# The first MLP product by seven products for eight, four tiles at once, in half of the features of blocks 2 to 6

## The chip, the cores and the metric

The kernel runs on one core of a Trainium2 chip. A core has five engines with a queue each, which work in the order of their queues and wait for one another by semaphores: TensorE (PE in the profile; its weight loads are PEld), VectorE (DVE), ScalarE (ACT), GpSimd (POOL) and SyncE (SP, which here only issues DMAs). Matrix products land in PSUM, 8 banks of 128 partitions by 512 words of 32 bits. The metric is the device time of one execution in microseconds (us), the median of three runs.

## The reference

An attention with random features is followed by an MLP. For q, k, v of shape (8 batches, 8 heads, 576 positions, 64) and omega of 128 x 64:

```python
q_p, k_p = phi(q * scale), phi(k * scale)      # exp(projection - norm - max), 128 features
num = q_p @ (k_p^T v);  den = q_p . sum(k_p)   # per batch and head
x = (num / den) as 4608 tokens x 512
h = x @ w_in                                   # 512 x 2048
g = h * clip(h + 3, 0, 6) / 6
out = g @ w_out                                # 2048 x 512
```

## The kernel before, in words

**Blocks and stages.** The tokens are worked in nine blocks of 512: block b (0 to 7) is the main 512 positions of batch b, block 8 holds the 64 left over of each batch. Stage b holds three things that the engines interleave: the attention of batch b + 1 (projections on TensorE, exponentials on ScalarE, maxima and divisions on VectorE, scaling of v on GpSimd or ScalarE), the first MLP product of block b, and the second MLP product of block b - 1.

**First product, eight for eight.** `mm1` (L1048 on) makes one tile of 128 features by 512 tokens: four matmuls of 512 columns at L1064 into one PSUM bank. ScalarE then makes relu(h/6 + 0.5) into `tsb` (L1070), and VectorE multiplies min(tsb, 1) with the bank into `gT` (L1072). A block has 16 such tiles.

**First product, seven for eight.** In blocks 7 and 8 `mm1_pair` is used instead (`FIRST7 = (7, 7)`, one number for each half of the features). It takes features f and f + 8 and both halves of the tokens as a 2 x 2 product and makes it with seven products of half the size in place of eight, from sums and differences of the tokens (`x_sums`: X1 to X4) and of the weights (`input_sums`: W1 to W4). It has 14 matmuls of 256 columns at L1143. Partial results are copied from one PSUM bank to another (or to `p7` in SBUF) by ScalarE or VectorE (256 columns each), and a later matmul adds onto the copy: [...]such a bank (`onto`) must have held a full tile. Two additions on VectorE (L1180, L1182) follow.

**Second product.** From block 1 on it is made with seven products for eight as well: `token_sums` and `last_sum` form S1 to S4 of `gT`, four sums for each quarter of the features, and `products` (L1322) has 7 x 16 matmuls of 256 columns. All sums of the kernel pass through `combine` (L1250). S1 to S4 run on GpSimd (`ADD`), except in the last block, where VectorE shares them.

**Order.** Each engine's order is written out by hand in `ORDER`, as numbers of operations. A small planner (`schedule`) walks these lists with assumed durations. It decides only which PSUM bank each tile gets and which semaphore waits are needed; the engines then run freely.

**Buffers.** The sums of weights and tokens for the first product lie in the space of `k32` and `q32`, which only batch 0 uses for its own data.

Of the kernel before, what the change touches and what calls it, by code (L numbers as in the profile page):

```python
# [14 lines left out]
IDLE_UNTIL = 21.0  # L15
EV0 = (("ACT","DVE"), ("ACT","DVE"), ("POOL", "ACT"), {"k": ("POOL", "ACT", "DVE"), "q": ("POOL", "ACT","DVE")})
# [6 lines left out]
        240, 223, 395, 396, 408, 238, 245, 401, 402, 403, 397, 225, 398, 213, 404, 409, 243, 410, 413, 416, 271, 198,  # L23
        419, 251, 228, 422, 425, 428, 291, 431, 434, 275, 273, 277, 279, 437, 303, 300, 440, 294, 309, 297, 306, 443,
        446, 449, 287, 289, 576, 315, 283, 596, 566, 567, 322, 597, 568, 330, 285, 312, 577, 281, 324, 578, 357, 569,
        326, 579, 328, 336, 318, 580, 320, 598, 332, 570, 344, 334, 581, 571, 586, 587, 346, 359, 349, 582, 362, 599,
        583, 383, 588, 370, 572, 589, 388, 375, 600, 372, 385, 352, 590, 591, 592, 365, 378, 601, 391, 593, 602, 603,
        614, 620, 573, 629, 493, 503, 505, 617, 632, 495, 623, 501, 466, 469, 472, 644, 635, 638, 499, 509, 653, 475,
        511, 507, 478, 650, 481, 490, 484, 647, 665, 487, 497, 659, 775, 668, 662, 519, 776, 521, 531, 785, 536, 524,
        533, 778, 779, 543, 708, 555, 545, 548, 786, 560, 557, 791, 788, 789, 688, 792, 794, 795, 701, 798, 799, 808,  # L30
        715, 802, 817, 820, 805, 811, 728, 832, 823, 733, 835, 740, 730, 826, 847, 841, 745, 838, 853, 742, 963, 856,
        752, 850, 754, 764, 979, 757, 964, 766, 973, 769, 966, 967, 974, 876, 976, 977, 980, 889, 982, 983, 993, 996,
        1005, 990, 1008, 999, 986, 987, 916, 1011, 896, 1023, 1020, 1014, 903, 1026, 928, 1029, 1041, 1035, 933, 930,
        1044, 940, 1151, 921, 1038, 945, 918, 1152, 952, 942, 1167, 957, 954, 1161, 1154, 1162, 1077, 1155, 1164,
        1165, 1064, 1168, 1170, 1171, 1084, 1184, 1181, 1193, 1178, 1187, 1174, 1175, 1091, 1202, 1104, 1199, 1214,
        1116, 1196, 1118, 1106, 1208, 1217, 1109, 1121, 1229, 1140, 1226, 1211, 1145, 1128, 1223, 1133, 1130, 1232,
        1339, 1349, 1340, 1142, 1355, 1265, 1342, 1343, 1350, 1272, 1356, 1352, 1353, 1381, 1369, 1372, 1384, 1366,
        1375, 1358, 1362, 1359, 1363, 1396, 1252, 1405, 1387, 1399, 1390, 1411, 1417, 1402, 1420, 1414, 1304, 1292,
        1527, 1297, 1279, 1528, 1294, 1306, 1309, 1543, 1316, 1537, 1318, 1530, 1321, 1531, 1538, 1328, 1453, 1330,
        1333, 1540, 1541, 1460, 1544, 1546, 1467, 1550, 1547, 1551, 1440, 1554, 1563, 1560, 1557, 1572, 1492, 1584,  # L40
        1497, 1494, 1480, 1575, 1482, 1485, 1516, 1569, 1518, 1504, 1590, 1509, 1521, 1506, 1587, 1578, 1593, 1605,
        1599, 1602, 1608, 1622, 1623, 1653, 1666, 1625, 1656, 1682, 1669, 1658, 1626, 1671, 1695, 1661, 1685, 1632,
        1674, 1687, 1711, 1698, 1633, 1700, 1724, 1690, 1714, 1635, 1716, 1636, 1703, 1727, 1753, 1740, 1719, 1729,
        1641, 1642, 1743, 1756, 1732, 1745, 1800, 1758, 1638, 1639, 1748, 1803, 1813, 1761, 1805, 1645, 1646, 1816,
        1808, 1829, 1818, 1769, 1770, 1832, 1842, 1821, 1834, 1858, 1772, 1845, 1773, 1847, 1837, 1861, 1779, 1871,
        1863, 1850, 1887, 1780, 1874, 1866, 1900, 1876, 1890, 1782, 1783, 1892, 1879, 1903, 1785, 1786, 1905, 1788,
        1895, 1789, 1908, 1932, 1916, 1917, 1792, 1793, 1926, 1927, 1919, 1920, 1929, 1930, 1933, 1951, 1936, 1937,
        1948, 1945,
    ],
    "SP": [  # L50
        0, 18, 22, 33, 20, 23, 26, 25, 24, 27, 28, 32, 29, 30, 31, 262, 260, 261, 465, 464, 462, 461, 463, 460, 459,
        687, 575, 393, 685, 585, 684, 686, 595, 539, 605, 527, 551, 563, 681, 682, 564, 683, 801, 873, 872, 874, 736,
        797, 869, 875, 748, 760, 772, 870, 773, 871, 1060, 989, 985, 1062, 1063, 1057, 1061, 936, 924, 1059, 960, 948,
        1058, 961, 1248, 1249, 1250, 1251, 1246, 1177, 1124, 1112, 1136, 1148, 1149, 1245, 1247, 1173, 1433, 1361,
        1365, 1436, 1438, 1439, 1437, 1312, 1300, 1435, 1324, 1336, 1337, 1434, 1549, 1500, 1553, 1488, 1524, 1512,
        1525, 1644, 1648, 1791, 1795, 1939, 1943, 1953, 1941, 1950,
    ],
    "ACT": [
        21, 19, 118, 139, 132, 148, 142, 160, 145, 136, 151, 128, 124, 154, 184, 167, 157, 134, 187, 202, 169, 175,
        173, 171, 163, 179, 232, 219, 177, 165, 234, 181, 209, 224, 399, 405, 411, 414, 214, 199, 417, 272, 229, 420,  # L60
        423, 252, 426, 292, 432, 429, 276, 435, 274, 278, 438, 301, 295, 310, 441, 298, 307, 444, 304, 288, 450, 284,
        447, 356, 323, 290, 316, 313, 286, 343, 282, 331, 358, 327, 337, 319, 325, 333, 321, 329, 335, 345, 381, 369,
        384, 584, 371, 353, 366, 379, 392, 604, 594, 615, 621, 574, 504, 494, 506, 618, 633, 496, 624, 502, 630, 470,
        467, 645, 636, 473, 639, 500, 654, 510, 476, 651, 482, 479, 485, 648, 518, 491, 666, 488, 660, 514, 530, 669,
        498, 520, 663, 508, 532, 777, 541, 512, 554, 780, 544, 711, 556, 714, 709, 713, 693, 689, 697, 695, 700, 694,
        691, 702, 706, 707, 704, 723, 699, 721, 809, 720, 803, 716, 821, 718, 727, 806, 812, 738, 833, 818, 824, 741,
        750, 827, 842, 836, 839, 751, 762, 848, 763, 753, 854, 851, 857, 965, 885, 879, 887, 882, 883, 877, 565, 890,
        892, 888, 911, 894, 994, 881, 997, 1006, 895, 991, 914, 1000, 1009, 1012, 897, 902, 899, 927, 901, 1021, 1015,
        904, 906, 1024, 909, 929, 1030, 939, 1027, 951, 1036, 1042, 908, 950, 1045, 1039, 1153, 953, 1082, 1078, 1080,
        1083, 1067, 1070, 1073, 1071, 1075, 1115, 1069, 1065, 1076, 1085, 1087, 1185, 1182, 1089, 1090, 1179, 1194,  # L70
        1102, 1092, 1188, 1203, 1105, 1094, 1097, 1200, 1117, 1197, 1127, 1215, 1096, 1139, 1209, 1218, 1212, 1129,
        1230, 1227, 1224, 1233, 1341, 1268, 1271, 1266, 1270, 1275, 1277, 1278, 1273, 1370, 1373, 1367, 1385, 1376,
        1382, 1397, 1255, 1253, 1261, 1263, 1388, 1257, 1264, 1259, 1303, 1400, 1391, 962, 1406, 1412, 1403, 1258,
        1418, 1291, 1421, 1415, 1314, 1282, 1280, 1315, 1285, 1529, 1284, 1326, 1532, 1329, 1458, 1459, 1454, 1456,
        1461, 1463, 1466, 1465, 1472, 1473, 1470, 1468, 1441, 1443, 1449, 1445, 1447, 1446, 1555, 1452, 1561, 1558,
        1564, 1493, 1515, 1479, 1573, 1451, 1481, 1576, 1517, 1585, 1505, 1570, 1579, 1588, 1594, 1591, 1600, 1606,
        1603, 1609, 1624, 1654, 1655, 1667, 1668, 1657, 1670, 1683, 1662, 1684, 1627, 1664, 1675, 1696, 1697, 1677,
        1699, 1712, 1713, 1691, 1693, 1715, 1704, 1725, 1726, 1720, 1706, 1728, 1741, 1754, 1742, 1733, 1755, 1722,
        1744, 1757, 1735, 1749, 1801, 1802, 1804, 1762, 1764, 1814, 1815, 1751, 1830, 1809, 1831, 1811, 1771, 1833,
        1822, 1843, 1844, 1838, 1859, 1846, 1860, 1824, 1774, 1840, 1862, 1851, 1872, 1873, 1853, 1875, 1889, 1869,  # L80
        1880, 1891, 1902, 1867, 1904, 1896, 1882, 1909, 1911, 1898, 1921, 1940, 1944, 1942, 1947,
    ],
    "DVE": [
        17, 6, 7, 8, 5, 12, 13, 16, 15, 122, 116, 120, 140, 149, 143, 146, 137, 185, 11, 182, 126, 152, 155, 200, 130,
        215, 161, 189, 158, 230, 204, 191, 192, 206, 207, 221, 194, 196, 222, 236, 211, 237, 197, 212, 239, 241, 249,
        246, 242, 250, 226, 247, 400, 406, 227, 412, 244, 415, 1614, 418, 424, 421, 1615, 427, 293, 430, 280, 436,
        433, 10, 338, 9, 439, 302, 296, 311, 299, 442, 445, 341, 305, 308, 354, 451, 448, 367, 1616, 606, 317, 314,
# [68 lines left out]
class Prog:  # L156
# [46 lines left out]
    def schedule(self):  # L203
# [57 lines left out]
        def slots_of(o):  # L261
            t, picks = 0.0, []
            for i, vx in enumerate(o.alloc):
                idle = sorted((0.0 if h is None else h.free_at, i) for i, h in enumerate(vx.ring.held)
                              if (h is None or h.left == 0) and (not vx.onto or (h is not None and h.full)))
                if len(idle) <= i:
                    return None
# [134 lines left out]
def _emit(nc, es, q, k, v, omega, w_in, w_out, out):  # L402
# [109 lines left out]
    def actt(n):  # L512
        return 0.07 + n / 1200.0
# [998 lines left out]
```

The softmax here doesn't subtract the row's maximum and nothing guards it: scores larger than these inputs give would overflow.

## Time and profile before

| | before |
|---|---|
| three runs | 301.58, 301.95, 302.17 us; median 301.95 |
| span of the profiled execution, first to last instruction | 300.0 us |
| first matmul starts, last one ends, after the span's start | 1.2 us, 297.0 us |
| mean granted TensorE clock | 1.000 |
| PE, DVE, ACT, POOL busy | 294.4, 243.2, 215.9, 232.0 us |
| L1064: 512-column matmuls | 384 |
| L1143: 256-column matmuls of blocks 7 and 8 | 224 |
| L1322: 256-column matmuls of the second product | 880 |
| L1250 on GpSimd, 128 x 512 sums | 1.16 us each |
| stages 2 to 6 | about 73 to 226 us of the span |

The profiled execution has no time of its own beside its span; the runs' median is 1.95 us above it, for what lies before the first and after the last instruction. In the page, a group's busy time is the union of its rows, so that overlap counts once, and its mean is the length of one row. In the 40 slices each digit is a tenth of busy share, and the "chain that ended last" follows the end of the kernel back from each instruction to what released it.

### The profile page before, as it was taken

To read this page: it belongs to the slowest core of one execution; us is meant where nothing else is said; L and a number is where in the kernel's file an instruction comes from. 1 tells how busy PE (TensorE), PEld (TensorE's weight loads), DVE (VectorE), ACT (ScalarE), POOL (GpSimd) and SP (SyncE) were. 2 spreads that over 40 slices of the span, in tenths; PEclk is the share of its full clock that TensorE was granted. 3 is DMA by queue.
4 is the path that set the end of the run, shared out by engine and by line. 5 is a ranking of instruction groups with operands and counts; after the bars stand their busy time and mean duration, and the time that the engine had idled before them with its cause. 6 is when DMAs were issued, how large, how long until landed. Compare 5 with 4: busy or idle time off the path is not lost.

```text
span 300.0 us, 7322 instructions
## 1 busy us (share of the span) xinstructions
PE 294.4 (98%) x2774; PEld 211.4 (70%) x2778; DVE 243.2 (81%) x530; ACT 215.9 (72%) x529; POOL 232.0 (77%) x247
## 2 busy tenths in 40 slices
PE   8899999999999999999999999999999999999995
PEld 6689955555785578556865586658755788888885
DVE  3978995689868886789778857887799999878985
ACT  3978998599959984989388644598875778687400
POOL 1774567088996979789889986989768999999960
PEclk9999999999999999999999999999999999999999
DMA  7999989999859997699839895999934100110024
GB/s 237 293 187 180 267 129 170 184 252 185 185 124 227 164 195 119 166 163 264 166 84 177 148 210 159 124 223 146 161 115 123 28 1 2 70 73 0 37 108 140
DMA packets 90099, 44.88 MB, mean 150 GB/s; under 512 B 57936, under 2 KB 87760, under 8 KB 90064
## 3 DMA queue, kind: packets, MB, share of 16 engines
q1 hardware_dynamic: 62352, 30.91, 44.3%
q0 software_dynamic: 26592, 12.46, 32.9%
q10 hardware_dynamic: 1120, 1.05, 1.1%
q8 instruction: 22, 0.36, 0.5%
q14 instruction: 13, 0.11, 0.1%
HBM read 36.73 MB, written 9.44 MB: 154 GB/s over the span
## 4 chain that ended last, share of the span: by engine, by line
PE 89%; DVE 7%; ACT 2%; issue 1%; DVEq 0%
PE p L1322 31%; PE p L1064 23%; PE p L1143 7%; PE p L1234 5%; PE p L1209 5%; DVE gT L1072 4%; PE p L995 3%; PE p L967 3%; PE p L777 2%; PE p L578 2%; PE p L780 2%; PE p L821 1%; PE p L703 1%; DVE wi L1250 1%; ACT kp L828 1%; PE p L841 1%
## 5 line engine op out<-in xcount | busy, mean ns | idle before, releaser
L1064 PE MATMUL p<-xT,wi 128*128 128x512 f16 x384 | 89.8, 379 | 0.1
L1072 DVE SCALAR_TENSOR_TENSOR gT<-tsb,p 128x512 f16<-128x512 f16 x96 | 62.4, 679 | 11.7 <-ACT tsb L1070 10.7
L1070 ACT ACTIVATE tsb<-p 128x512 f16<-128x512 f32 x96 | 55.3, 611 | 16.6 <-PE p L1064 13.2
L1064 PEld LDWEIGHTS p<-xT,wi 128*128 128x128 f16 x384 | 35.8, 98 | 38.5 <-issue 1.3
L1322 PE MATMUL p<-wo,gT 128*128 128x256 f16 x368 | 45.6, 273 | 0.0
L1322 PEld LDWEIGHTS p<-wo,gT 128*128 128x128 f16 x368 | 34.9, 98 | 6.3 <-issue 1.3
L1250 POOL TENSOR_TENSOR gT<-gT,s 128x512 f16<-128x512 f16 x30 | 34.7, 1157 | 5.2 <-PE p L1322 3.0
L1250 POOL TENSOR_TENSOR gT<-gT 128x512 f16<-128x512 f16 x31 | 36.1, 1165 | 2.8 <-DVE gT L1072 0.5
L1250 POOL TENSOR_TENSOR s<-gT 128x512 f16<-128x512 f16 x30 | 34.8, 1159 | 4.1 <-DVE gT L1072 1.5
L1250 POOL TENSOR_TENSOR s<-gT,s 128x512 f16<-128x512 f16 x31 | 35.8, 1156 | 2.6 <-DVE gT L1072 0.4
L796 ACT ACTIVATE kp<-p 128x512 bf16<-128x512 f32 (+1 forms) x50 | 26.2, 562 | 11.0 <-PE p L780 11.0
L801 DVE TENSOR_REDUCE mx<-kp 128x4 f32<-128x512 bf16 (+1 forms) x50 | 29.7, 620 | 4.0 <-ACT kp L796 3.6
L805 ACT ACTIVATE qpT<-p 128x512 bf16<-128x512 f32 (+1 forms) x50 | 27.1, 567 | 7.7 <-PE p L780 7.7
L1322 PE MATMUL p<-t,gT 128*128 128x256 f16 x256 | 31.6, 273 | 0.0
L951 POOL TENSOR_TENSOR vc<-v,cc 128x512 bf16<-128x512 f32 x22 | 23.3, 1059 | 8.3 <-DMA v<-in_v_dram 3.0
L524 ACT COPY p<-p 128x256 f32<-128x256 f32 (+1 forms) x51 | 19.8, 400 | 12.8 <-PE p L1143 6.6
L624 POOL DMA_DIRECT2D qb<-in_q_dram x28 | 19.6, 711 | 11.2 <-PE p L1064 10.4
L1011 DVE TENSOR_TENSOR xb<-p,rec 128x256 f16<-128x256 f32 (+1 forms) x64 | 28.0, 470 | 0.2
L1322 PEld LDWEIGHTS p<-t,gT 128*128 128x128 f16 x256 | 24.3, 98 | 4.2 <-issue 1.3
L1191 ACT ACTIVATE tsb<-p 128x512 f16<-128x512 f32 x32 | 19.1, 604 | 4.2 <-PE p L1143 1.6
L1193 DVE SCALAR_TENSOR_TENSOR gT<-tsb,p 128x512 f16<-128x512 f16 x32 | 21.3, 679 | 0.5 <-ACT tsb L1191 0.3
L624 POOL DMA_DIRECT2D kb<-in_k_dram x21 | 16.2, 784 | 6.0 <-PE p L1064 6.0
(135 smaller groups left out, 578.7 us busy)
## 6 DMA issues: line engine op xcount, KB each, us to landing
v<-in_v_dram SPq DMA_DIRECT2D x14, 512.0 KB, 4.9
out_dram<-osb SPq DMA_DIRECT2D x14, 512.0 KB, 3.4
kb<-in_k_dram POOLq DMA_DIRECT2D x14, 256.0 KB, 5.2
qb<-in_q_dram POOLq DMA_DIRECT2D x14, 256.0 KB, 5.4
wo<-in_moe_w_out_dram POOLq DMA_DIRECT2D x8, 256.0 KB, 8.3
wi<-in_moe_w_in_dram POOLq DMA_DIRECT2D x3, 512.0 KB, 7.5
q<-in_q_dram SPq DMA_DIRECT2D x4, 256.0 KB, 4.7
vl<-in_v_dram SPq DMA_DIRECT2D x8, 128.0 KB, 3.8
```

Of the source, the lines that this page charges most:

```text
L624: lambda E: E.dma_start(dst, src), prio + 0.001 * turn_of[0], reads=gate, writes=keys,
L796: op("ACT", actt(128 * (d1 - d0)), lambda E, lh=lh, ko=ko, part=part: E.activation(ko, out_of(part, 0, lh)[0].rearrange("p (x m) -> p x m" ...
L801: op("DVE", dvet(128 * (d1 - d0)), lambda E, ko=ko, mo=mo: E.reduce_max(mo, ko, axis=AX.X), p0 + 0.01, reads=[("kp", 0, d, lh) for d in ra ...
L805: op("ACT", actt(128 * (d1 - d0)), lambda E, lh=lh, part=part: E.activation(qd[:, part[0]:part[1], lh, :], out_of(part, 1, lh)[0].rearrang ...
L951: return E.tensor_tensor(vcm[:, :, 0:D], v32[:, m, :, :], cbc, ALU.mult)
L1011: op("DVE", dvet(128 * n), lambda E: E.tensor_tensor(xv(i0, i1), psum()[:, :, :, 0:64], rbc, ALU.mult), t + 0.01, reads=[vn, ("rec", ru)], ...
L1064: ins = E.matmul(ring.t[vh.slot], wi[:, c, 128 * f:128 * f + 128], xv[:, c, :], start=(c == 0), stop=(c == NJ - 1))
L1070: op("ACT", actt(512), lambda E: E.activation(tsb[tu][:], ring.t[vh.slot], AF.Relu, bias=0.5, scale=1.0 / 6.0), t - 0.1, reads=[vh], write ...
L1072: op("DVE", dvet(512), lambda E: E.scalar_tensor_tensor(gT[gu][:, f, :], tsb[tu][:], 1.0, ring.t[vh.slot], ALU.min, ALU.mult), t - 0.1, re ...
L1193: op("DVE", dvet(512), lambda E, v=v, tu=tu, dst=dst: E.scalar_tensor_tensor(dst(), pieces(tsb[tu][:]), 1.0, pieces(v.ring.t[v.slot]), ALU ...
L1250: op(engines, {"POOL": 0.07 + n / 455.0, "DVE": 0.1 + n / 850.0}, lambda E: E.tensor_tensor(dst, x, y, ALU.subtract if minus else ALU.add) ...
L1322: ins = E.matmul(ring.t[v.slot][:, 256 * j:256 * j + 256], a[:, f, 128 * j:128 * j + 128], w[:, f, :], start=(first and f == 0 and j == 0) ...
```

## The change

- `FIRST7` becomes (7, 2): the second half of the features (f = 4 to 7 and 12 to 15) uses seven products for eight from block 2 on; the first half still from block 7. Its weight sums (`input_sums(1)`) are made during stage 1.
- A new function, `mm1_quad`, does this for two neighbouring f at once. Two features, each with its partner f + 8, and both halves of the tokens make four tiles of 512 words: X, Y, Z and W, each a full PSUM bank. It has seven steps of four matmuls of 256 columns. Three evictions of 512 columns (q1 and q2 into the banks Y and Z, q3 into `p7`, now 512 wide) and two additions of 512 columns on VectorE (q4, q5) take the place of the pair's smaller ones. `QUAD = (7, 2)` sends blocks 7 and 8 through it too, so `mm1_pair` is no longer called.
- Where no bank with a full tile is free, the bank is first filled by a clearing matmul (`washed`).
- `ADD` becomes ("POOL", "DVE"): every S sum and X sum may stand on GpSimd or VectorE, as `ORDER` says. In the new order, of the sums of `combine` in stages 2 to 6, 64 stand on GpSimd (80 before) and 36 on VectorE (none before). Eighteen of the value scalings (`vc`) of these stages stand on GpSimd (12 before), 2 on ScalarE (8 before).
- `ORDER` is new for all engines. The planner's assumed durations are altered, and it now treats GpSimd's operations and VectorE's sums as excluding each other (`port`).

```diff
-    FIRST7 = (7, 7)
+    FIRST7 = (7, 2)
+    QUAD = (7, 2)
+    SEVEN0 = False
...
-    p7 = [sbt("p7_%d" % u, [128, 256], F32) for u in range(2)]
+    p7 = [sbt("p7_%d" % u, [128, 512], F32) for u in range(2)]
...
+    def washed(E, v):
+        if v is not None and v.wash:
+            E.matmul(ring.t[v.slot], fill[:, 0:128], fill[:], start=True, stop=True)
+
+    def mm1_quad(blk, f):
+        u, gu = blk % 2, blk % 2
+        b = quarters(blk)
+        X, Y, Z, W = Virt(ring, True), Virt(ring, True, True), Virt(ring, True, True), Virt(ring, True)
...
+        def four(v, w, x, start=False, under=None):
+            def e(E):
+                washed(E, under)
+                for g in range(2):
+                    for c in range(2):
+                        ins = E.matmul(bank(v)[:, 256 * g:256 * g + 256], w(c, f + g), x[:, c, :],
+                                       start=start and g == 0 and c == 0, stop=c == 1, skip_group_check=True)
+                return ins
+            return e
...
+        op("PE", each, four(X, orig(0, 0), b[0][0], True, Y), ..., name="qa." + nm)
+        op(EV_O, both(512), evac(lambda: bank(Y), lambda: bank(X)), ..., name="q1." + nm)
+        op("PE", each, four(W, summed(W3s), X3s[u], True), ..., name="qw." + nm)
+        op(EV_O, both(512), evac(lambda: p7[w7][:], lambda: bank(W)), ..., name="q3." + nm)
+        op("PE", each, four(X, orig(0, 1), b[1][0]), ..., name="qb." + nm)
+        op("PE", each, four(Y, summed(W2s), X2s[u], under=Z), ..., name="qy." + nm)
+        op(EV_O, both(512), evac(lambda: bank(Z), lambda: bank(Y)), ..., name="q2." + nm)
+        op("PE", each, four(Z, summed(wi[:, 0:2, 1024:2048]), X1s[u]), ..., name="qz." + nm)
+        op("DVE", dvet(512), lambda E: E.tensor_tensor(bank(Y), bank(Y), p7[w7][:], ALU.add), ..., name="q4." + nm)
+        op("PE", each, four(Y, orig(1, 1), X4s[u]), ..., name="qc." + nm)
+        op("DVE", dvet(512), lambda E: E.tensor_tensor(bank(W), bank(Z), p7[w7][:], ALU.add), ..., name="q5." + nm)
+        op("PE", each, four(Z, summed(W4s), b[1][1]), ..., name="qd." + nm)
+        for n, (v, i, k_) in enumerate(((X, 0, 0), (Y, 1, 0), (W, 1, 1), (Z, 0, 1))):
...
-    ADD = ("POOL",)
+    ADD = ("POOL", "DVE")
...
                 if seven(blk, 2 * g):
-                    for f in (2 * g, 2 * g + 1):
-                        mm1_pair(blk, f)
+                    if QUAD[g // 2] <= blk:
+                        mm1_quad(blk, 2 * g)
+                    else:
+                        for f in (2 * g, 2 * g + 1):
+                            mm1_pair(blk, f)
```

The loop at the end of `mm1_quad` is the same pair of steps as in `mm1`, on ScalarE and VectorE, for each of the four banks.

## The prediction

> **What bounds the kernel now.** I read the page's busy shares and slices first, to see whether any engine is full and when.
>
> ```profile
> PE 294.4 (98%) x2774; PEld 211.4 (70%) x2778; DVE 243.2 (81%) x530; ACT 215.9 (72%) x529; POOL 232.0 (77%) x247
> PE   8899999999999999999999999999999999999995
> POOL 1774567088996979789889986989768999999960
> PEclk9999999999999999999999999999999999999999
> PE 89%; DVE 7%; ACT 2%; issue 1%; DVEq 0%
> ```
>
> TensorE is full from the third slice to the last but one, at the full clock, and the chain that ended last is TensorE for 89%. A busy TensorE may still hide gaps, so next the stretches of stages 2 to 6, which the change touches (the columns are length, PE, PEld, DVE, ACT and POOL busy with counts, then clock, DMA share, GB/s):
>
> ```profile
> 104.00:134.00 30.00, 29.98 (x277) 19.73 (x276) 23.34 (x51) 22.96 (x63) 24.89 (x27) 1.00 0.98 164
> 134.00:164.00 30.00, 30.00 (x302) 20.26 (x301) 24.47 (x56) 23.45 (x61) 26.98 (x29) 1.00 0.93 170
> 73.00:226.00 153.00, 152.93 (x1497) 102.66 (x1497) 122.07 (x276) 116.48 (x303) 130.40 (x137) 1.00 0.90 165
> ```
>
> 0.07 us of 153 is idle on TensorE: five stages of about 30.6 us. Last, the timeline of TensorE, for what one matmul occupies (start, length, instructions):
>
> ```profile
> 61.41 1.89 PE L1064 MATMUL p<-xT,wi 128*128 128x512 f16 x8
> 63.14 0.27 PE L841 MATMUL p<-qT,om 128*128 128x256 bf16 x1
> ...
> 290.65 1.91 PE L1322 MATMUL p<-wo,s 128*128 128x256 f16 x16
> 292.40 0.27 PE L1322 MATMUL p<-t,gT 128*128 128x256 f16 x1
> ```
>
> Eight 512-column matmuls take 63.14 - 61.41 = 1.73 us, 0.216 each; sixteen 256-column ones 1.75 us, 0.109 each. The means of the groups (379 and 273 ns) include the drain that the next matmul overlaps, so they are not used.
>
> **What the skill says.** "TensorE: Matmul & The Clock Gate", section "Wait — 56ns, not 53.3ns?", gives N / 2.4 GHz plus about 2.5 ns when warm: 215.7 and 109.2 ns. The trace agrees (216, 109). "VectorE: DVE Perf Modes", section "The perf-mode tier table", caps tensor_tensor at 2x for 16-bit operands in SBUF and at 1x with PSUM: a sum of 512 half floats should be cheap on VectorE, an addition in PSUM not. "SBUF — State Buffer", section "SBUF: two separate sides", says that a VectorE instruction with two SBUF inputs and a GpSimd instruction that reads SBUF exclude each other, for a whole instruction. Both show in the timeline of VectorE, then GpSimd:
>
> ```profile
> 282.84 0.68 DVE L1338 TENSOR_TENSOR osb<-p 128x512 f32<-128x512 f32 x1
> 283.44 0.42 DVE L1250 TENSOR_TENSOR s<-gT 128x512 f16<-128x512 f16 x1
> 283.78 1.27 DVE L1193 SCALAR_TENSOR_TENSOR gT<-tsb,p 128x512 f16<-128x512 f16 x2
> 285.09 1.35 DVE L1250 TENSOR_TENSOR s<-gT 128x512 f16<-128x512 f16 x1
> ```
>
> ```profile
> 285.02 1.15 POOL L1250 TENSOR_TENSOR gT<-gT 128x512 f16<-128x512 f16 x1
> 286.24 1.21 POOL L1250 TENSOR_TENSOR s<-gT,s 128x512 f16<-128x512 f16 x1
> ```
>
> Start to start, an addition with PSUM takes VectorE 0.60 us and a sum 0.34; the sum at 285.09 starts 0.07 after a GpSimd sum and takes 1.35, ending 0.27 after it. A collision so costs VectorE up to about 1 us.
>
> **The change, part by part.** *TensorE.* By the order of instructions, 160 matmuls of 512 columns go and 280 of 256 come (10 groups of four tiles, 28 each, in blocks 2 to 6); no clearing matmul is issued, so every seeded bank had been full. 160 x 0.216 = 34.6 us less, 280 x 0.109 = 30.5 more, one more filler 0.1: net -3.9 us, 0.8 a stage. Blocks 7 and 8 keep their 224 matmuls. Weight loads stay hidden: L1322 already streams at 0.109 with one each.
>
> *VectorE, blocks 2 to 6.* Twenty additions in PSUM, 20 x 0.60 = 12.0 us; 36 sums that GpSimd did or that are new, 36 x 0.345 = 12.4 if nothing holds the port; evictions and small copies that trade places with ScalarE, about -1. By start-to-start times a stage held 23.3 us before (16 gT at 0.60, ten maxima 5.4, output additions 3.3, divisions 3.2, the rest small): 116.5 for five, and about 140 after. TensorE after needs 153 - 3.9 = 149. So VectorE, 76% full before, is 94% full, with 149 - 140 = 9 us, or 0.26 us a sum, for port waits.
>
> *ScalarE.* 28 evictions of 512, 28 x 0.48 = 13.4 us; six value scalings of eight instructions leave for GpSimd, -6 x 1.9 = -11.5; small moves +3. 110 becomes about 116 of 149: no bound, but its queue is in order (below).
>
> *GpSimd.* 16 fewer sums, -16 x 1.16 = -18.6; six value scalings, 6 x 1.06 = +6.4: 140 becomes about 127. Their consumers on TensorE stand 10 us and more behind: nothing on the path. The DMA issues keep their number; two last stores pass from SyncE to ScalarE, after its work, at about nothing.
>
> *Blocks 7 and 8.* 48 evictions of 256 columns become 24 of 512, 32 additions become 16: ScalarE saves about 2 us, VectorE 1. TensorE is 29.93 of 30 us busy from 240 to 270, so this buys nothing; without that cover it could be worth some tenths.
>
> *The four weight sums* of this half move to stage 1 (4 x 0.6 us on VectorE, before the first group, which stands mid-stage 2), hidden by VectorE's slack there.
>
> **Where it can come back.** A group needs its seed: first product, eviction by ScalarE (0.59), then the product that adds to it. I walked ScalarE's and VectorE's queues through the new order, adding the times above from the TensorE instruction that frees a queue's next work to the one that waits for its end, with 0.2 us for each signal (in the trace ScalarE's waiting L1070 rows start that long after their tile's last matmul has streamed). The tightest places are behind the bursts of projections: in stage 4, ScalarE's 19 instructions after the second burst end 0.8 us after TensorE would want the freed bank for the fourth matmul tile; 0.6, 0.5 and 0.5 in stages 3, 5 and 6. The old order walked the same way is late by 0.5, 0.1, 0.5 and 0.3, where the trace shows almost no idle TensorE. I charge the excess, +1.0 us. If the signals are faster it is 0; if each place is charged whole, +2.4.
>
> For the port: in stage 3 the order runs VectorE without rest for 17 us, up to the additions of the first group, with three X sums in it. Those stand where GpSimd has finished its S4 and X3 sums and issues its seven DMAs (7 x 0.7 us), which leave the port free; stage 4 does the same. So I take few collisions, under 0.1 us a sum and within the slack: 0. The other end: the sum that met a busy GpSimd in the profile waited 0.7 us on average (twelve cases, 0.05 to 1.1), GpSimd holds the port for two thirds of a stage, 0.48 us a sum, 17 us in all.
>
> Sum: -3.9 + 1.0 = -2.9. The profiled span of 300.0 becomes 297.1; the median of the runs is 1.95 above that span, work outside the first and last instruction that the change leaves alone. Prediction 299.0 us.
>
> **Rivals.** *The gain is given back* at tight places: all walked lateness is real (+2.4) and VectorE's collisions take another 1 us: 301.95 - 3.9 + 3.4 = 301.4. For it: TensorE loses its freedom where ScalarE and VectorE are full. Against: the old order had such places and no stalls.
>
> *VectorE becomes the bound, slower.* Sums collide as if unplanned: 140 + 17 = 157 us for stages that took 153: 301.95 + 4 = 306. It decides from 0.37 us of waiting a sum (13 / 36). For it: 94% load on an in-order queue. Against: the sums' places beside DMA issues, and GpSimd's lower load.
>
> *More than the sum*: the new sequence also mends the first 20 us, where TensorE waits 1.9 us now: 297. Little speaks for it; the order there is nearly the old one.
>
> *No saving at all* is excluded: the matmuls are counted in the order.
>
> **How the numbers follow.** Likeliest case 60%, own range 297.6 to 300.8 (stalls 0 to 2.4, rounded out). Given back 15%, 300.8 to 302.6: faster, same and slower in about equal parts. Slower 21%, 302.6 to 308. More than the sum 4%. Faster by over 0.2% (0.6 us, about what this kernel's runs can tell): 0.60 + 0.04 + 0.04 = 0.68; same 0.06; slower 0.26. The range 297.3 to 303.5 leaves out about half of the 4% and 60% of the 21%.
>
> **What would show it.** Right: L1064 falls to 224 matmuls; the groups' 280 run at 0.109; TensorE stays over 29.7 of 30 us busy in stages 2 to 6; VectorE's L1250 sums mean under 0.55 us; the chain stays TensorE's by over 85%. Wrong: tenths of TensorE fall to 8 in the middle slices, with waits on gT or on the additions (VectorE, port) or on banks after the bursts (ScalarE); sums that mean 0.8 us or more point to the port.

## The result and the profile after

| | before | after |
|---|---|---|
| median of the runs | 302.2 us (12 runs) | 302.1 us (12 runs, 301.05 to 303.26) |
| ratio after to before, 95% interval | | 0.9995 (0.9978 to 1.0011) |
| span of the profiled execution | 300.0 us | 300.6 us |

Two of the executions reported further down ran at a lower granted clock (309.96 us at 0.95, 336.68 us at 0.854) and count in no median or ratio.

The change makes no difference that can be measured; 299.0 us had been forecast. The case that came true is the rival "the gain is given back", though only partly by the mechanism that it named.

The same rows of the page as before, of the changed kernel (busy shares, TensorE and GpSimd in 40 slices, the granted clock, the chain that ended last):

```profile
PE 292.2 (97%) x2899; PEld 222.1 (74%) x2899; DVE 271.4 (90%) x593; ACT 212.9 (71%) x479; POOL 206.3 (69%) x226
PE   7999999999999999999989999999999999999996
POOL 1664827039898986589939869998279939869711
PEclk9999999999999999999999999999999999999999
PE 81%; DVE 8%; ACT 5%; POOL 5%; issue 1%; POOLq 0%
```

TensorE's slices fell to 8 in one place in the middle, and the chain passes through VectorE, ScalarE and GpSimd for 18% of the span, where it was 9%. The stretches of stages 2 to 6 (length, PE, PEld, DVE, ACT, POOL busy with counts, clock, DMA share, GB/s):

```profile
104.00:134.00 30.00, 30.00 (x319) 22.47 (x317) 28.51 (x66) 23.93 (x61) 22.08 (x25) 1.00 0.97 162
134.00:164.00 30.00, 28.19 (x299) 20.57 (x298) 27.23 (x57) 22.55 (x50) 23.60 (x25) 1.00 1.07 174
73.00:226.00 153.00, 150.97 (x1577) 111.63 (x1576) 144.65 (x322) 119.95 (x278) 119.61 (x126) 1.00 0.96 164
```

Between 73 and 226 us TensorE now idles 2.0 us (0.07 before), nearly all of it in stage 4, and VectorE is busy for 144.65 of 153 us (122.07 before). The timeline of TensorE shows what one matmul occupies and where it stops (the bracket is what the profile names as the releaser of the idle time):

```profile
151.19 0.38 PE L799 MATMUL p<-qT,om 64*128 64x512 bf16 x2
152.93 3.40 PE L1083 MATMUL p<-xT,wi 128*128 128x512 f16 x15 [1.37 <-ACT qpT L824]
...
157.02 1.90 PE L1083 MATMUL p<-xT,wi 128*128 128x512 f16 x8
158.76 0.60 PE L1248 MATMUL p<-xT,wi 128*128 128x256 f16 x4
159.20 1.03 PE L1083 MATMUL p<-xT,wi 128*128 128x512 f16 x4
160.65 1.04 PE L1083 MATMUL p<-xT,wi 128*128 128x512 f16 x4 [0.42 <-DVE gT L1091]
...
238.04 1.03 PE L1415 MATMUL p<-t,s 128*128 128x256 f16 x8 [0.67 <-POOL s L1343]
...
281.01 1.05 PE L1415 MATMUL p<-t,gT 128*128 128x256 f16 x8 [0.42 <-DVE u L1431]
```

Eight plain matmuls still take 158.76 - 157.02 = 1.74 us, and four of the groups' take 159.20 - 158.76 = 0.44, 0.11 each: the matmuls cost what was forecast. But the four from 159.20 on should be followed at 160.06 (4 x 0.216), and the next begins at 160.65: 0.59 us lost. By the same reckoning, start to start, TensorE loses 1.43 us ahead of 152.93 (the last two matmuls of a burst of projections, here those at 151.19, are followed 0.31 us on where nothing waits; the expectations below count this wait as 1.53), 0.83 ahead of 238.04 and 0.58 ahead of 281.01. Smaller ones are 0.32 at 94.1, 0.30 at 27.8, 0.23 at 165.9, 0.09 at 148.7, and 0.27 before the first matmul (it starts at 1.45 us, not 1.19, because VectorE first clears the fill tile, which the change widened from 256 to 512 columns). These make 4.64 us; the two such waits that only the kernel before had, at 116.5 and 241.8, were 0.33. So 300.0 - 3.9 + 4.64 - 0.33 = 300.4, within 0.2 of the span of 300.6: the saving is there, and new waits of about the same size are there too. What causes them is the question of the experiments.

Two views speak for the port that VectorE and GpSimd share. VectorE's sums by shape (name, count, total us, mean ns, idle before):

```profile
L1343 DVE TENSOR_TENSOR s<-gT,s 128x512 f16<-128x512 f16 x11 | 7.0, 639 | 0.1
L1343 DVE TENSOR_TENSOR s<-gT 128x512 f16<-128x512 f16 x13 | 6.4, 492 | 0.0
L1343 DVE TENSOR_TENSOR gT<-gT,s 128x512 f16<-128x512 f16 x11 | 5.6, 512 | 0.5 <-PE p L1415 0.5
L1343 DVE TENSOR_TENSOR gT<-gT 128x512 f16<-128x512 f16 x8 | 5.0, 629 | 0.0
L1343 DVE TENSOR_TENSOR q<-xT,q 128x512 f16<-128x512 f16 x5 | 3.2, 633 | 0.0
```

An unhindered one takes 0.415. All 55 of 512 columns in the kernel mean 0.56, so 0.15 us a sum is spent waiting; 15 of them took over 0.5. One of these, in the timeline of VectorE and then of GpSimd:

```profile
278.34 0.69 DVE L1286 SCALAR_TENSOR_TENSOR gT<-tsb,p 128x512 f16<-128x512 f16 x1 [0.94 <-ACT tsb L1284]
278.94 1.41 DVE L1343 TENSOR_TENSOR s<-gT,s 128x512 f16<-128x512 f16 x1
280.28 0.68 DVE L1431 TENSOR_TENSOR u<-p 128x512 f32<-128x512 f32 x1
```

```profile
277.69 2.38 POOL L1343 TENSOR_TENSOR gT<-gT,s 128x512 f16<-128x512 f16 x2
```

This sum (S28.1: S2 of block 8, quarter 1) ends at 280.35, 0.28 us after GpSimd's second sum (277.69 + 2.38 = 280.07); the addition behind it in the queue is the one that TensorE waits for at 281.01. That is the exclusion of the Trainium skill's "SBUF — State Buffer", section "SBUF: two separate sides", by one whole instruction.

### The profile page after: what moved, and what is told of

The parts are those of the page before. It is cut to its first block, busy times and chain, and to the rows that moved or that the text cites. A ratio compares the mean times of both kernels' runs of the same rounds, so it can differ in the third digit from the quotient of the medians.

```text
span 300.6 us, 7551 instructions
## 1 busy us (share of the span) xinstructions
PE 292.2 (97%) x2899; PEld 222.1 (74%) x2899; DVE 271.4 (90%) x593; ACT 212.9 (71%) x479; POOL 206.3 (69%) x226
## 3 DMA queue, kind: packets, MB, share of 16 engines
q10 hardware_dynamic: 1408, 1.25, 1.3%
## 4 chain that ended last, share of the span: by engine, by line
PE 81%; DVE 8%; ACT 5%; POOL 5%; issue 1%; POOLq 0%
PE p L1415 29%; PE p L1248 15%; PE p L1083 11%; PE p L1327 5%; PE p L1302 4%; PE p L1014 3%; PE p L986 2%; DVE mx L820 2%; PE p L796 2%; POOL s L1343 2%; PE p L597 2%; ACT kp L847 2%; PE p L860 2%; POOL vc L970 1%; PE p L840 1%; PE p L799 1%
## 5 line engine op out<-in xcount | busy, mean ns | idle before, releaser
L1083 PE MATMUL p<-xT,wi 128*128 128x512 f16 x224 | 53.1, 379 | 1.8 <-ACT qpT L824 1.4
L1415 PE MATMUL p<-wo,gT 128*128 128x256 f16 x368 | 47.0, 273 | 0.0
L1083 PEld LDWEIGHTS p<-xT,wi 128*128 128x128 f16 x224 | 21.3, 98 | 24.9 <-ACT qpT L824 2.1
L543 ACT COPY p<-p 128x512 f32<-128x512 f32 x55 | 32.2, 599 | 4.1 <-PE p L1415 2.0
L970 POOL TENSOR_TENSOR vc<-v,cc 128x512 bf16<-128x512 f32 x27 | 28.7, 1061 | 7.1 <-DVE cc L964 5.2
L1343 POOL TENSOR_TENSOR gT<-gT,s 128x512 f16<-128x512 f16 x21 | 24.3, 1157 | 12.0 <-PE p L1415 10.6
L1343 POOL TENSOR_TENSOR gT<-gT 128x512 f16<-128x512 f16 x24 | 28.2, 1177 | 4.7 <-DVE s L1343 3.2
L1030 DVE TENSOR_TENSOR xb<-p,rec 128x384 f16<-128x384 f32 (+1 forms) x64 | 28.2, 467 | 0.3
L1343 POOL TENSOR_TENSOR s<-gT,s 128x512 f16<-128x512 f16 x21 | 24.4, 1164 | 3.4 <-DVE s L1343 2.2
L1343 POOL TENSOR_TENSOR s<-gT 128x512 f16<-128x512 f16 x19 | 22.0, 1158 | 4.7 <-DVE gT L1286 3.1
```

Source lines behind the costliest of these rows:

```text
L543: return E.copy(dst(), src())
L970: return E.tensor_tensor(vcm[:, :, 0:D], v32[:, m, :, :], cbc, ALU.mult)
L1083: ins = E.matmul(ring.t[vh.slot], wi[:, c, 128 * f:128 * f + 128], xv[:, c, :], start=(c == 0), stop=(c == NJ - 1))
L1343: op(engines, {"POOL": 0.1 + n / 475.0, "DVE": 0.09 + n / 2000.0}, lambda E: E.tensor_tensor(dst, x, y, ALU.subtract if minus else ALU.add ...
L1415: ins = E.matmul(ring.t[v.slot][:, 256 * j:256 * j + 256], a[:, f, 128 * j:128 * j + 128], w[:, f, :], start=(first and f == 0 and j == 0) ...
```

## The experiments

Three theories stood. The gain went to *the sums* (VectorE's sums collide on the port, GpSimd's come late; the expectations call these P and G), to *ScalarE behind the bursts of projections* (A, the releaser that the profile names at 152.93, and what the prediction had charged), or to something for which the profile names ScalarE wrongly, first of all *the DMA transposes that bring x into `xT`* (D). All times below stand beside runs of the kernel before on the same chip, with medians of 302.06 to 302.26 us. Gains on the changed kernel are against its 302.1 us above; it was not run again beside these.

| run | median, us (runs) | ratio to before, 95% interval |
|---|---|---|
| VectorE's sums cut | 300.22 (6) | 0.9944 (0.9928 to 0.9959) |
| GpSimd's sums cut | 299.79 (5) | 0.9926 (0.9915 to 0.9938) |
| exponentials cut | 301.58 (22) | 0.9976 (0.9967 to 0.9985) |
| fill of 256 columns | 301.82 (22) | 0.9975 (0.996 to 0.999) |
| block 4 reads `wo` | 300.97 (8) | 0.9954 (0.9939 to 0.997) |
| all sums cut | 299.87 (6) | 0.9916 (0.9894 to 0.9937) |
| four moves | 301.62 (22) | 0.9973 (0.996 to 0.9985) |
| kernel before, sums cut | 302.0 (13) | 1.0 (0.9984 to 1.0017) |
| six moves with the store | 303.46 (22) | 1.0037 (1.0021 to 1.0052) |
| the store alone | 303.46 (21) | 1.0039 (1.0023 to 1.0055) |
| moves again | 299.97 (5) | 0.9928 (0.9908 to 0.9947) |
| sums cut, block 4 reads `wo` | 298.71 (5) | 0.9874 (0.9851 to 0.9897) |

### The sums, on one engine and on both

The edit is one line in `combine`; the first sums of each kind stay whole, so that every buffer holds data. For VectorE:

```diff
+            w = 16 if late and E is nc.vector else dst.shape[-1]
-            dst, x, y, ALU.subtract if minus else ALU.add)
+            dst[:, :, 0:w], x[:, :, 0:w], y[:, :, 0:w], ALU.subtract if minus else ALU.add)
```

> The changed kernel with VectorE's S and X sums cut to 16 of each 256 columns (S1 and S4 from block 1, S2 and S3 from block 3, X from block 4 on; the sums' other columns are left out, GpSimd's sums are whole). Theory P (VectorE is late because its sums collide with GpSimd on the port, and by their own 0.34 us): the waits of TensorE at 159.8 and 280.3 us of the profile (0.6 each) go, and part of those at 151 and 237: 1.5 to 3 us faster than the changed kernel, near 299.5. Theory A (ScalarE's queue behind the bursts of projections): at most 0.5 us faster, near 302. A cut sum still waits for a GpSimd instruction that holds the port, so the part that stays is collision, the part that goes is VectorE's own work.

For GpSimd, `E is nc.gpsimd`:

> The changed kernel with GpSimd's S and X sums cut to 16 of each 256 columns (same blocks as in the run before; the other columns are left out, VectorE's sums are whole). Most of what can hold the port, and GpSimd's own lateness, are gone. Theory P: VectorE's sums fall to a mean of 0.41 us, the waits at 159.8, 237 and 280.3 go: 1.5 to 2.5 us faster than the changed kernel. Theory G (only GpSimd's queue is late, at the second product of block 6): 0.8 us faster. Theory A: 0 to 0.5 us faster; the 1.5 us at 151 stay.

And for both:

> Leaves work out: every S and X sum on both engines, the first ones of each kind apart, makes 16 columns in place of 512 or 1024. All that is left is the change's matmuls, evictions and additions. If the sums (port, VectorE's fill, GpSimd's lateness) take all of the gain, the time falls to the predicted saving and past it by nothing: 298.0 (302.1 less 3.9, with the wait at 151 left or not, 297.7 to 299). If the two engines' sums cost separately (1.9 and 2.3 us when each alone is cut), 297.9; if they are the same loss counted twice, 299.7, no less than the cut of GpSimd's alone.

Measured: 1.9 us less than the changed kernel without VectorE's sums, 2.3 without GpSimd's, 2.2 without either. The two don't add up: it is one loss, which each cut removes from its own side. With GpSimd's cut, VectorE's sums stay whole and mean 0.45 us, only 4 of them over 0.5, and TensorE's waits at 94, 159.8, 237 and 280 are gone. With VectorE's cut, those at 94 and 280 are gone, but 0.33 us stays of the one at 159.8 and 0.58 of the one at 237, where TensorE waits for GpSimd's sums: they are late even with VectorE's cut to 16 columns. So the sums' meeting on the port and GpSimd's own lateness cost 2.2 us together; the runs do not split the two. The wait at 151 is absent from the profiles of the first two runs and 1.22 us long in that of the third, so it is not the sums that bring it.

The control is the same cut in the kernel before:

> The kernel before, with GpSimd's S sums cut to 16 columns of 512 (the first ones of each kind and the X sums of blocks 7 and 8 left whole). Leaves that work out. If the sums cost nothing before the change, because TensorE stood full with room ahead of it, the time stays within 0.5 us of 302.2; the 2.3 us that the same cut gains after the change are then the change's own. If the sums held the kernel before as well, it gains 1 us or more, and the 2.3 us say little of the change.

302.0 us, ratio 1.0 (0.9984 to 1.0017): there the sums cost nothing that can be measured. The 2.2 us are the change's own, not a debt that the kernel had already.

### What TensorE waits for at 152.93

Theory A, the exponentials of block 5, with a quarter of their columns each:

> The changed kernel with the exponentials of batch 5 alone (k and q, stage 4) cut to 32 of 128 columns; the rest of their output is left out. ScalarE has about 7 us less to do in stage 4 and frees the banks behind the bursts sooner. Theory A: the waits of TensorE at 151.2 (1.5), 146 and 148.7 (0.3) go and the one at 159.8 may: 1.5 to 2.4 us faster than the changed kernel, near 300. Theory P or G: 0 to 0.5 us.

The time falls 0.5 us, and a wait of 1.06 us (start to start) stays at that place. ScalarE's exponentials are not what holds it; at most the 0.5 is their part. In this profile the wait at 159.8 is gone as well, and one of 0.38 at 165.3 is new. ScalarE so has a share in a wait that goes with the sums too, and the 0.5 may overlap with their 2.2.

Theory D. In `mm1`, for block 4 alone:

```diff
+        if blk == 4:
+            xk, xv = [("wo", 0), ("wo", 1)], wo
```

> Other data: the eight plain tiles of block 4 (first half of the features) take the first four columns of wo as their tokens in place of x transposed; the instructions, shapes and order stay, only the wait for the DMA transposes of x before these eight tiles is gone. Theory D (the 1.53 us at 151.2 is a wait for the last DMA transpose of block 4, although the profile names ScalarE): the wait is gone, 0.1 us or less, and the time falls by 0.5 to 1.5 us, to about 301.1; the other waits (159.8, 237.1, 280.3) stay. Theory A (TensorE waits for ScalarE's exponentials behind the second burst, as the profile names it): the wait of 1 to 1.5 us stays, and the time is 302.1.

TensorE's timeline in this run, the second burst and the first product of block 4:

```profile
151.54 0.38 PE L799 MATMUL p<-qT,om 64*128 64x512 bf16 x2
151.85 3.63 PE L1085 MATMUL p<-wo,wi 128*128 128x512 f16 x16
```

The product follows the burst at once (151.85 - 151.54 = 0.31 us, the same as between these two in the kernel before), with ScalarE's work unchanged. The median falls by 1.1 us and the runs spread over 0.7 us (8 runs) in place of 2.2 (12). This one profile could not decide by itself, since its last transpose had landed by 150.88. Two others do. In the changed kernel's, the last transpose landed at 152.84, and TensorE began at 152.93. In that of the run with both causes gone, below, it landed at 152.59, and TensorE, reading `wo`, had begun at 151.78. So the profile had named ScalarE for a wait that ended with a DMA. What it says of the tile `xT` from 140 to 156 us, first before the change, then after (duration in ns and first and last start; issue to landing in us):

```profile
L1040 SPq DMA_TRANSPOSE xT<-xb x4: 1188/1191/1266, 142.3 to 147.3; - x4
DMA to landing us min/median/max: 3.4/3.8/4.4
```

```profile
L1059 SPq DMA_TRANSPOSE xT<-xb x4: 1254/1338/1806, 143.2 to 148.2; - x4
DMA to landing us min/median/max: 2.5/3.5/4.6
```

Before, the last of the four is issued at 147.3, and TensorE comes to block 4's first product at 153.96: 6.7 us for a landing that takes up to 4.4. After, the last issue is at 148.2 and TensorE would have come at about 151.5: 3.3 us. The first transpose needs the divisions of its columns, which stand on VectorE behind five gT steps and end at 143.04; the others follow it one by one on SyncE. The last is issued 0.9 us later than before, and TensorE comes 2.5 us sooner. That VectorE's sums make the transposes late is not shown: with all sums cut, the last was issued at 148.96. A landing of 2.5 us is in time, one of 4.6 isn't. In the twelve profiles of the changed kernel and its variants this last transpose landed 2.4 to 2.5 us after its issue (seven) or 4.0 to 4.6 (five), never between; what decides is open. So the same order waits there in one execution and not in the next. That is a part of the spread of the runs, not all of it: the kernel before spreads from 301.5 to 304.2 us in 43 runs without this wait.

The fill tile:

```diff
-    fill = sbt("fill", [128, 512], BF16)
+    fill = sbt("fill", [128, 256], BF16)
```

> The changed kernel with the tile for filler matmuls 256 wide again, as before (nothing in this order reads more). The first matmul of the changed kernel starts 0.27 us later than before, behind the memset of that tile. If that is a cost on the path: 0.3 us faster than the changed kernel. If the start-up waits for loads anyway: no difference.

0.3 us less, and the first matmul starts at 1.19 us again. The earlier start is seen directly; a gain of 0.3 in the time is not clear of the noise, since the two intervals overlap (0.996 to 0.999, and 0.9978 to 1.0011 for the changed kernel). The runs lie between 300.15 and 302.61. The profiled one took 300.16, which is 2.3 us less than the profiled run of the changed kernel (302.46), with the same order. The fill is 0.27 of this. Its last transpose landed after 2.48 us, and the wait at 151 (1.43) is absent; so is the one at 280 (0.58). The sum S28.1 starts 1.25 us behind the start of GpSimd's first sum in both profiles; here it takes 0.42 us, not 1.41, and GpSimd's two sums take 2.68, not 2.38: this time GpSimd waited. Collisions, too, come and go from one execution to the next.

### Both causes gone at once

> Leaves out the sums as in e6 (16 columns) and takes other data for block 4's plain tiles as in e5, with the narrower fill: both suspected causes gone at once. If the sums (port and GpSimd's lateness) and the transposes of block 4 are the whole of what ate the gain, all 3.9 us of TensorE arrive: 297.8 to 298.4, with no wait of TensorE over 0.4 us after the first 20 us. If something else holds too, or if the waits are one loss in two places, it stays at 299.5 or above, no less than with the sums alone.

298.71 us, by 3.35 us less than the kernel before it ran beside (302.06). The stretch of stage 4, of stages 2 to 6, and the chain in this run:

```profile
134.00:164.00 30.00, 29.98 (x318) 22.58 (x317) 27.08 (x63) 23.65 (x52) 13.68 (x28) 1.00 1.11 177
73.00:226.00 153.00, 152.98 (x1608) 113.80 (x1607) 139.06 (x327) 122.22 (x285) 76.74 (x132) 1.00 0.97 165
```

```profile
PE 96%; ACT 2%; DVE 1%; issue 0%
```

TensorE idles 0.02 us of 153 again. Against the changed kernel the run gains 3.4 us, and the parts that were measured one by one are 2.2 (sums), 1.1 (block 4) and 0.3 (fill), 3.6. By the ratios to the kernel run beside each they are 4.2 and the whole 3.7; each part is known to about half a microsecond, so they add up as far as can be told. The run leaves out the sums' own work, so its time is no goal for the whole computation. The expectation's lower figure, 297.8 to 298.4, was missed by 0.3; waits of 0.30 at 28 and 0.09 at 149 remain, which are new with the change too and which no run took away; what they wait for is open.

### Moving the work

In the names that follow, P6.2 is the product number 2, counted from 0, of block 6's second MLP product, made in two halves of eight matmuls; S26.1 is the sum S2 of block 6, quarter 1; X4.4 is the sum X4 of block 4; u3.7 is an addition in block 7's second product; R5.2 is the burst number 2 of batch 5's projections; qb.7.0 is the step `qb` of `mm1_quad` in block 7.

Four moves by what each wait in the trace named (the engine first, then the operation):

```diff
+PE:   P6.1 (first half) ahead of P6.2;  P3.4 (first half) behind the burst R5.2
+DVE:  u3.7 ahead of S28.1
+POOL: S13.0 ahead of X1.4
+fill of 256 columns
```

> The whole computation. Four moves in the order and a narrower fill: P6.1 before P6.2 on TensorE (P6.2 waited 0.83 us for GpSimd's S2 sums at 237), u3.7 before S28.1 on VectorE (0.58 at 280), S13.0 before X1.4 on GpSimd with P3.4 earlier on TensorE (0.58 at 159.8), the fill tile 256 columns wide (first matmul 0.27 earlier). If the waits that the trace shows are each the loss they look like, 0.83 + 0.58 + 0.4 + 0.27 come back: 300.0, and below 299.3 where the wait at 151 stays away. If a stalled TensorE only meets the next late engine, the waits turn up one or two steps later, at the products after P6.1 and at the last tiles, and the time is 301 to 302.

301.62: only 0.2 us below the narrower fill alone, which is within the noise. The wait at 280 is gone, those at 94 and 159.8 stay (0.32, 0.58). The wait at 237 had moved on, as the second forecast said. VectorE, GpSimd and TensorE in this run:

```profile
238.28 1.21 DVE L1343 TENSOR_TENSOR s<-gT,s 128x512 f16<-128x512 f16 x1
239.41 1.27 DVE L1286 SCALAR_TENSOR_TENSOR gT<-tsb,p 128x512 f16<-128x512 f16 x2
```

```profile
238.06 1.15 POOL L1343 TENSOR_TENSOR q<-xT 128x512 f16<-128x512 f16 x1
```

```profile
240.15 1.05 PE L1415 MATMUL p<-wo,gT 128*128 128x256 f16 x8 [0.49 <-DVE gT L1286]
```

The sum S26.2 meets GpSimd's X1.7 and ends late, the gT steps queued behind it are late, and the second half of P6.1 now waits for those: where P6.2 had waited for GpSimd, P6.1 waits for VectorE. So the next version moved the colliding sums themselves, and the store that stood ahead of block 4's transposes on SyncE:

```diff
+DVE:  S41.1 to S41.2;  X4.4 behind the gT step of tile 4.3;  S26.2 to S26.3;  u3.7 ahead of S28.1
+POOL: S26.1 ahead of S36.2
+SP:   the store outw.2.1 behind the four transposes Xdma.4
+fill of 256 columns
```

> The whole computation. The order of the changed kernel with the narrower fill and six moves: on VectorE the sums S41.1, X4.4 and S26.2, which waited 0.8 to 1.0 us beside GpSimd's work, stand behind the additions and gT steps that TensorE waits for, and u3.7 stands before S28.1; on GpSimd S26.1 stands before S36.2; on SyncE the store outw.2.1 stands behind the four transposes of x of block 4. If single collisions and the late transposes, in these places, are what eats the gain, the waits at 94, 151, 159.8, 237 and 280 go or halve, and the time is 299.3 to 300.3. If the stalls only move to the next late engine, as they did when the products were moved, it stays at 301.2 or above.

and, as the only move, the store:

> The whole computation, the changed kernel with one move: on SyncE the store outw.2.1 (1.1 us of issue) stands behind the four transposes of x of block 4, not ahead of them. Theory D, the transposes of block 4 come late: each is issued up to 1.1 us earlier, the wait at 151 is 0.4 us or none, and the time falls by 0.5 to 1.1, to about 301.2, in a narrower spread. If the transposes are held by the divisions that fill their source, and not by the store ahead of them, nothing changes: 302.1.

Both are slower than either kernel, 303.46. Neither forecast for the store had this. SyncE, then VectorE, with the store alone moved:

```profile
143.02 6.04 SPq L1059 DMA_TRANSPOSE xT<-xb  x4
149.11 0.57 SPq L1511 DMA_DIRECT2D out_dram<-osb  x1
```

```profile
154.01 0.69 DVE L1431 TENSOR_TENSOR osb<-p 128x512 f32<-128x512 f32 x1 [3.37 <-DMA out_dram<-osb]
```

The first transpose begins at 143.02 in place of 143.20 and the last at 147.87 in place of 148.24, far less than the 1.1 us that the store takes to issue: in the main it had not held them. But the store reads `osb`, and the next output addition writes it. Issued at 149.1 and landed 4.9 us later, it stops VectorE's whole queue for 3.37 us. TensorE's wait at 151 is gone, and waits of 0.33, 1.33, 0.90 and 0.77 us follow between 154 and 163. In the run with six moves another is instructive (VectorE, then TensorE):

```profile
94.64 2.28 DVE L1343 TENSOR_TENSOR gT<-gT,s 128x512 f16<-128x512 f16 x2
```

```profile
97.58 1.69 PE L1083 MATMUL p<-xT,wi 128*128 128x512 f16 x7 [0.97 <-DVE gT L1091]
```

S41.1, moved from 88.7 to stand beside S41.2, waits there as well, and now right ahead of a gT step that TensorE needs: 1.13 us lost where it had been 0.32. What a collision costs depends on what stands behind it in the queue, and that is why the place counts.

The last version takes the moves of both versions but those of P6.1, of S41.1 and of the store, and adds one of qb.7.0:

```diff
+PE:   P3.4 (first half) behind R5.2;  qb.7.0 ahead of P6.2 (second half)
+DVE:  X4.4 behind the gT step of tile 4.3;  S26.2 to S26.3;  u3.7 ahead of S28.1
+POOL: S26.1 ahead of S36.2;  S13.0 ahead of X1.4
+fill of 256 columns
```

> The whole computation. The changed kernel's order with the narrower fill and these moves, the store left in its place: u3.7 before S28.1, X4.4 behind four gT steps and S26.2 before S26.3 on VectorE; S26.1 before S36.2 and S13.0 before X1.4 on GpSimd; P3.4's first half behind the second burst and qb.7.0 before P6.2's second half on TensorE. The moves that paid where they were tried, without the store and without S41.1. If the waits they took away stay away, about 0.4 at 159, 0.8 at 237, 0.6 at 280 and the one at 151 against the kernel with the narrower fill alone (301.8): 299.8 to 300.6. If stalls move on: 301.2 to 301.8.

299.97 us, 0.9928 (0.9908 to 0.9947) of the kernel before: faster than both kernels, with the whole computation. Its five runs lie between 299.64 and 300.26. The fastest run of the narrower fill alone, 300.15, lies among them, so what the moves brought is fewer executions with long waits, not a faster best one. Its stages 4 and 2 to 6, and its chain:

```profile
134.00:164.00 30.00, 29.88 (x314) 21.77 (x312) 27.59 (x61) 23.36 (x52) 25.00 (x27) 1.00 1.04 178
73.00:226.00 153.00, 152.56 (x1585) 112.16 (x1583) 144.74 (x324) 121.43 (x281) 121.23 (x128) 1.00 0.95 164
```

```profile
PE 84%; DVE 11%; ACT 3%; DMA 1%; issue 0%
```

VectorE is as full as in the changed kernel (144.74 and 144.65 us) and 13 of its sums still take over 0.5 us; but TensorE idles 0.44 us here in place of 2.03. No wait at 151 shows, but the last transpose landed after 2.48 us, so this profile does not try P3.4's move. That of the four moves does: there it landed at 152.91, TensorE was busy with P3.4's eight matmuls from 152.07, and block 4's first product began at 153.00, with less than 0.1 us lost. With VectorE's load the same and nearly as many collisions, TensorE stood still for 1.6 us less: what counts here is where they stand and what each can delay. The moves were not tried one by one, so how much each brings is open.

## Why the prediction was wrong, step by step

- **TensorE, -3.9 us: right.** The counts and the 0.109 us a matmul are as forecast, and with the two causes gone 3.35 us arrive in the time.
- **VectorE, 94% full with 0.26 us of slack a sum: right as a mean, and the step from it to "0" is what failed.** The sums wait 0.15 us each, within the slack, and 144.65 us of 153 is no bound. But a wait isn't spent as a mean: ten of the 55 sums wait 0.5 to 1.0 us each, in an in-order queue, ahead of steps that TensorE needs within a microsecond. The prediction compared sums over a stage where it should have asked for every sum what stands behind it.
- **"Those stand where GpSimd ... issues its seven DMAs", under 0.1 us a sum: wrong as to where they stand.** The premise held: the seven sums of the profile beside GpSimd's DMA issues alone took 0.39 to 0.42 us. But 24 stood beside nothing and 24 beside a sum or scaling of GpSimd, three of them beside an issue as well; all 15 that took over 0.5 us are among these 24, so 0.15 us a sum came where under 0.1 had been taken. The order was read as if both queues would run at the times that were walked; they run freely, and a small shift decides: X4.4 took 1.33 us where it started 1.17 us ahead of the recorded start of GpSimd's S13.0, and 0.41 in the run with fewer exponentials, 1.29 ahead.
- **GpSimd, "nothing on the path": wrong.** P6.2 waited 0.83 us at 237 for S2 sums. GpSimd had idled 5.7 us up to 217.8 for the transposes of block 6, and with sums and scalings in one queue was busy nearly without a rest from 223 to 238. With VectorE's sums cut it still waited 0.58, so this is in the main GpSimd's own lateness, not the port's. A busy sum of a stage said nothing on that. With the collisions, this is the 2.2 us that the prediction put at 0.
- **ScalarE behind the bursts, +1.0: too high.** Cutting its exponentials brought 0.5. The place in stage 4 was right and its cause was not: the walk followed ScalarE and VectorE, and left out SyncE's transposes, which the divisions on VectorE release. That step is missing from the sum, and is worth 1.1 us.
- **The fill of 512 columns** was not costed: the first matmul starts 0.27 us later.
- **Small slips.** 6 x 1.9 is 11.4, not 11.5, so ScalarE's sum is 115, not 116; 13 / 36 is 0.36, not 0.37. Nothing hangs on them.
- **The rivals.** "Given back" came to 301.4 with ScalarE's lateness at 2.4 and collisions at 1; the runs put 0.5 and 2.2 there, and 1.1 on transposes that no rival named. That its figure came within 0.7 us of the result is in part luck. VectorE as the bound, slower, did not come: it was said to decide from 0.37 us of waiting a sum, and 0.15 was measured.

Of "what would show it", the 224 matmuls and 0.109 came true; TensorE over 29.7 of 30 us (28.19 in stage 4), sums under 0.55 (0.56) and a chain over 85% (81%) did not, and the fall of a middle slice to 8 was the sign given for wrong.

## What to carry to other kernels

When work is taken off a full engine, the others must be early enough for it at every place, not in the mean: list, for each wait that can be long (a shared port, a DMA), what stands behind it in its queue and how soon the full engine needs that. Follow the chain through DMAs and the buffers that they read, too; the profile may name an engine that had long been done, and giving the reader other data tells the two apart. A store moved later holds its buffer longer, and may stop the engine that writes it next. And one profile is one execution: the same order may show a wait in one and not in the next, so a wait's absence from a single profile is no proof that an edit removed it.

## What the hardware showed

- Which of two colliding sums waits, VectorE's or GpSimd's, can change between two executions (S28.1: 1.41 and 0.42 us, above).
- A sum on VectorE (X4.4 in the changed kernel, 158.33 to 159.66) took 1.33 us where the profile shows GpSimd at DMA issues until 159.5 and at its sum S13.0 until 160.71. With GpSimd's sums cut, the issues lay across it in the same way, and it took 0.41. So GpSimd's sum has a part in it, not the issues alone. But X4.4 ended 1.05 us ahead of that sum's recorded end, where S28.1 ended 0.28 after one. GpSimd's rows may be about a microsecond late there; no run settles it.
- Four transposes of one block take 2.5 to 4.6 us from issue to landing within one profile: a spread of over half the 3.9 us that the change was to save.
